# Scale and shift rows made side by side, biases in an early wait, and block 1's statistics ahead of the first queries, in the prologue of an adaLN attention + MLP kernel

## The chip, the cores and the metric

One core of a Trainium2 chip. The metric is the device time of one execution in microseconds (us), median of several executions. Engines are named as in the profile: PE is TensorE, DVE VectorE, ACT ScalarE, POOL GpSimd, SP the engine that issues nearly all DMAs.

## What is computed

One transformer layer on 2048 rows of width 512 in float32: attention with 32 query heads of 16 numbers that share one key head and one value head, then an MLP of width 1376. Both get their input through a layer norm whose scale and shift come from a vector `c`:

```python
mod = silu(c) @ w_mod                      # six rows of 512: sa, ca, ga, sb, cb, gb
h = layernorm(x) * (1 + ca) + sa
q, k, v = h @ wq, h @ wk, h @ wv           # 32 query heads, one key and value head
o = softmax(q @ k.T / 4) @ v               # for every head
x = x + ga * (o @ wo)
h = layernorm(x) * (1 + cb) + sb
out = x + gb * (gelu(h @ w1 + b1) @ w2 + b2)
```

## The kernel before

Attention is done in 64 units, each four heads of 256 query rows. The main loop (from `for u in range(NU)`) interleaves three things on PE: the scores of unit u (`e`, L685, exponentials on ACT in `p`), their product with the values (`acc`, L706), and, one to two units ahead, a first pass over the scores that only finds each row's maximum (`m`, L580, one `TENSOR_REDUCE` on DVE per product, L585). The rest (query projections, output projection, MLP) is fed in between in batches. The change leaves this loop alone.

All of the change is in the **prologue**, which ends where the first `e` product starts. Its order is written out by hand: each engine runs its instructions in the order of the code, and an engine whose next instruction waits holds up all that is behind it. x is worked in four blocks of 512 rows (`xt0` to `xt3`). Operands of accurate products are split in a high and a low part (`...H` on ACT, `...L` by subtraction on DVE or POOL), and a product is three matmuls: high by high, low by high, high by low.

The steps and their names:

- **Modulation rows.** `mod_row` (L308) multiplies `csb` (silu of c, 32 equal columns) with a half of a `w_mod` tile: `i` = 1 is the scale ca, `i` = 0 the shift sa. The two go to rows 32 to 63 and 0 to 31 of the bank `modrow`. ACT copies them to `modr` (L1373, L1384), `turn_rows` (L312) turns them to columns in `modc`. The scale half of `w_mod` is loaded ahead, the shift half after the first piece of `wq` (`load_mod`, L242). The scale is made first, then the shift, one matmul behind each row tile of block 0.
- **Block 0.** `stats1` (L406) makes mean and variance on DVE (`BATCH_NORM_STATS2`) and `rs`, `nm` on POOL; `xhat1` (L414) normalizes four tiles; `turn1` (L427) turns them by PE to the banks `tp`; `split1` (L433) makes `h0H`, `h0L`.
- **Biases.** `sab` holds the shift columns; `bias_row` (L370) multiplies it with `wq` and `wk`, giving the constant part of queries, keys and values (`biases`; for the other three query groups `bqs`, in `bias_rest`, L382, four matmuls of 384 columns).
- **First queries and keys.** `q_group` and `keys` (L1354, L1341) give the first 128 query columns (`qps`) and the keys and values of a block (`kps`). `place_q` (L532) puts the queries of unit 0 in place by selection products, `kv_out`, `low_k`, `repeat_k` (L451 to L468) write the keys to `ks` on ACT, DVE, ACT.
- **Blocks 1 to 3.** Normalized on ACT or POOL (`xhat1`), turned, copied from the bank by ACT (`x32`, L441), split by ACT and POOL (`bigH`, `bigL`).
- **Slots.** `SLOTS` (L25) is a table that sets the rest: a number n is n `m` products (`chunk`), a name is a step: "x 2" normalizes block 2, "heads 2" turns and splits one column tile of it, "keys 2" three matmuls of its keys, "low 2" and "k 2" the second and third write of the keys, "v 2" turns its values, "wq 1" scales and splits the second 128 query columns, "q 1" one quarter of the second queries, "rows" four modulation rows of the late part. From slot number `WIDE` on, every second `m` uses one of the three `e` banks; before that all `m` share three banks (tag "m", bufs=3), so the fourth `m` waits for the reduction of the first.

`FIRST_MAX` (L24) sets the order of the `m` products of units 0 and 1: (unit, key block) = (0,0), (1,0), (0,1), (1,1), (0,2), (0,3), (1,2), (1,3), eight products each. Only when all of unit 0's are reduced does `put_max` (L604) turn the maxima (DVE), gather and split them (POOL, `mt`, `mh`, `ml`) and send them by DMA into the rows of `qst` from which the first `e` products read. `keep_warm` (L290) issues matmuls on `wkH` whose results nobody reads.

Of the kernel before, what the change touches and what calls it, by code (L numbers as in the profile page):

```python
# [21 lines left out]
LEAD = 6  # L22
LEAD_0 = 6
FIRST_MAX = ((0, 0), (1, 0), (0, 1), (1, 1), (0, 2), (0, 3), (1, 2), (1, 3))  # L24
SLOTS = ((2, "x 2"), (2, "keys 1"), (2, "keys 1"), (2, "keys 1"), (2, "x 3", "keys 1"),  # L25
# [4 lines left out]
         (2, "rows"), (2, "rows", "wq 3"), (2, "rows", "load"), (2,))  # L30
WIDE = 16
MAX_WAIT = (1, 4)
QBUFS = 4
PREP = 4
# [22 lines left out]
def adaln_mqa_mlp(  # L57
# [182 lines left out]
    wms = [pro.tile([P, 2, D], F32, name=f"wm{k}", tag="wm", bufs=4) for k in range(KD)]  # L240

    def load_mod(i):  # L242
        for k in range(KD):
            nc.sync.dma_start(out=wms[k][:, i, :], in_=w_mod[k * P:(k + 1) * P, i * D:(i + 1) * D])

    load_mod(1)
# [17 lines left out]
    load_mod(0)  # L264
    load_x(1)
    load_x(2)
    load_x(3)
# [37 lines left out]
        for i, part in enumerate(wm):  # L305
            nc.tensor.matmul(ps[32 * i:32 * i + 32, :], csb[:, k, :], part, start=k == 0, stop=k == KD - 1)  # L306

    def mod_row(ps, i, k):  # L308

        nc.tensor.matmul(ps[32 * i:32 * i + 32, :], csb[:, k, :], wms[k][:, i, :], start=k == 0, stop=k == KD - 1)  # L310

    def turn_rows(ps, rows, i, n):  # L312
        for k in range(n):
            nc.tensor.transpose(ps[:, k, :], rows[32 * i:32 * i + 32, k * P:(k + 1) * P], ident[32 * i:32 * i + 32, 32 * i:32 * i + 32])

    pad(pro, 64, "pad2")
    wkH = pro.tile([P, KD, P], F32R, name="wkH")
# [29 lines left out]
    def scaled(dst, w, eng=nc.gpsimd):  # L347
        eng.tensor_tensor(out=dst, in0=w, in1=ca1.unsqueeze(2).to_broadcast([P, KD, P]), op=ALU.mult)
# [12 lines left out]
    def split_wq(g):  # L361
        gs = slice(g * P, (g + 1) * P)
        for j in range(2):
            src = wqms[g].rearrange("p k (a j r) -> p k a j r", j=2, r=16)[:, :, :, j, :]
            dh = wqH[:, :, gs].rearrange("p k (a r j) -> p k a j r", j=2, r=16)[:, :, :, j, :]
            dl = wqL[:, :, gs].rearrange("p k (a r j) -> p k a j r", j=2, r=16)[:, :, :, j, :]
            nc.scalar.copy(dh, src)
            nc.gpsimd.tensor_tensor(out=dl, in0=src, in1=raw(dh), op=ALU.subtract)

    def bias_row(ps, w):  # L370
        for k in range(KD):
            nc.tensor.matmul(ps, sab[:, k, :], w[:, k, :], start=k == 0, stop=k == KD - 1)

    def take_q(dst, ps):

        nc.scalar.copy(dst.rearrange("p (a r j) -> p a j r", j=2, r=16), ps.rearrange("p (a j r) -> p a j r", j=2, r=16))

    def prep_wq(g):
        scale_wq(g)
        split_wq(g)  # L380

    def bias_rest():  # L382

        n = KD - 1
        ps = psum.tile([P, n * P], F32, name="bqs", tag="x")
        row = pro.tile([32, n * P], F32, name="bqr", tag="h32", bufs=4)
        bias_row(ps[:32], wqf[:, :, P:D])
        for i in range(n):
            take_q(row[:, i * P:(i + 1) * P], ps[:32, i * P:(i + 1) * P])
# [24 lines left out]
    def xhat1(b, eng, n=QT):  # L414

        mv, rs, nm = hts_stats[b]
        xt = xts[b]
        for t in range(QT):
            eng = eng if t < n else nc.gpsimd
            if eng is nc.scalar:  # L420
                nc.scalar.activation(xt[:, t, :], xt[:, t, :], AF.Identity, scale=rs[:, t:t + 1], bias=nm[:, t:t + 1])
            else:
                eng.tensor_scalar(out=xt[:, t, :], in0=xt[:, t, :], scalar1=mv[:, t, 0:1], scalar2=rs[:, t:t + 1],
                                  op0=ALU.subtract, op1=ALU.mult)
            yield
# [7 lines left out]
    def split1(b, d):  # L433

        hH, hL = hts[b]
        ps = tps.pop((b, d))
        if b == 0:
            split(hH[:, d, :], hL[:, d, :], ps, act, dve)
        else:
            x32 = pro.tile([P, BQ], F32, name=f"x32_{b}_{d}", tag="h32", bufs=4)  # L440
            nc.scalar.copy(x32, ps)  # L441
            split(hH[:, d, :], hL[:, d, :], x32, act, pool)
# [927 lines left out]
    psc = psum.tile([P, 2, KD, 32], F32, name="modc", tag="v")  # L1370
    for k in range(KD):
        mod_row(psr, 1, k)
    nc.scalar.copy(modr[32:64], psr[32:64])  # L1373
    turn_rows(psc[:, 1], modr, 1, KD)
    nc.scalar.activation(ca1, psc[:, 1, :, 0], AF.Identity, bias=1.0)
    wqms[0] = pro.tile([P, KD, P], F32, name="wqm0", tag="wqm", bufs=1)
    for k in range(KD):
# [6 lines left out]
    nc.scalar.copy(modr[0:32], psr[0:32])  # L1384
    turn_rows(psc[:, 0], modr, 0, KD)
    spread_wkv()
    scaled(wkm, wk0, dve)
    load_constants()
    nc.vector.tensor_copy(out=sab, in_=psc[:, 0, :, 0:1].to_broadcast([P, KD, 32]))
    for d in range(KD):  # L1390
        split1(0, d)
    group = q_group()
    run(group, 1)
# [10 lines left out]
    nc.vector.tensor_copy(out=bq[:, 0:1], in_=psb[:, 2, 0:1])  # L1404
    nc.vector.tensor_copy(out=vbias, in_=psb[:, 3, 0:1])
    nc.vector.scalar_tensor_tensor(out=kbias, in0=psb[:, 3, 0:1], scalar=kkeep, in1=kmin, op0=ALU.mult, op1=ALU.add)

    def first_q(t):
        if t == 1:
            run(group)  # L1410
            load_q(1)

    stats1(1, first_q)
# [266 lines left out]
```

## Time and profile before

| | us |
|---|---|
| median of 3 runs (1571.49 to 1572.98) | 1572.91 |
| the profiled execution | 1574.09 |
| its span in the profile | 1572.3 |
| PE / DVE / ACT / POOL busy | 1556.0 / 1396.5 / 1232.0 / 680.6 |
| first `m` product starts | 31.62 |
| first `e` product starts (the prologue's end) | 91.52 |
| first `acc` product starts | 95.26 |

The profiled execution took 1.8 us more than its span, and 1.2 us more than the median of the runs. The prologue is 6% of the span; from 95 us on PE is busy in every stretch of 5 us. A row of the timeline has the start, the busy time of the group, engine, line, operation, tiles (out<-in), shapes and count, and in brackets the idle time of the engine just before it with what ended it. PEld is the load of a matmul's stationary operand.

### The profile page before, as it was taken

Reading aid. Unit: us, or ns where it says so; the run is one execution under the profiler, and the core shown is the slowest. Engines: PE = TensorE matmul, PEld = TensorE weight load, DVE = VectorE, ACT = ScalarE, POOL = GpSimd, SP = SyncE. Lnnn points to the kernel's source line nnn. Section 1 sums busy time; section 2 is a strip of 40 time slices with the busy share of each in tenths; the row PEclk is TensorE's granted clock in tenths of the full one; section 3 lists DMA queues with packets and bytes.
Section 4 is the critical chain, followed back from the end, with each engine's and each line's share of the span. In section 5 each row is a group of like instructions: output and inputs, shape, how many; then the busy total and the mean of one; then the engine's idle time right before and its main releaser. Section 6 shows DMA issues by size and latency. Waiting matters only on the chain.

```text
span 1572.3 us, 41712 instructions
## 1 busy us (share of the span) xinstructions
PE 1556.0 (99%) x16478; PEld 964.5 (61%) x16478; DVE 1396.5 (89%) x2490; ACT 1232.0 (78%) x2413; POOL 680.6 (43%) x1209
## 2 busy tenths in 40 slices
PE   8899999999999999999999999999999999999999
PEld 5445555556655676556655576556655676566658
DVE  5689999999999999999999999999999999999914
ACT  4657778778877888788877888778877888778874
POOL 3536452776521573235702474225721574146511
PEclk9999999999999999999999999999999999999999
DMA  7115521413112130302112130212202130203141
GB/s 255 66 47 178 179 79 54 144 47 98 45 48 79 45 98 16 110 17 87 55 42 86 35 107 17 86 51 62 89 26 76 45 116 26 83 28 100 48 148 48
DMA packets 83975, 120.65 MB, mean 77 GB/s; under 512 B 21294, under 2 KB 56686, under 8 KB 83524
## 3 DMA queue, kind: packets, MB, share of 16 engines
q1 hardware_dynamic: 83764, 117.99, 23.4%
q8 instruction: 130, 2.13, 0.6%
q14 instruction: 65, 0.53, 0.1%
q10 hardware_dynamic: 16, 0.00, 0.0%
HBM read 90.67 MB, written 26.74 MB: 75 GB/s over the span
## 4 chain that ended last, share of the span: by engine, by line
PE 87%; DVE 7%; DMA 0%; issue 0%; DVEq 0%; ACT 0%; SPq 0%
PE acc L706 30%; PE m L580 25%; PE e L685 16%; PE w1ps L202 8%; DVE mx L585 6%; PE w2ps L202 2%; PE w2ps L192 2%; PE qps L202 1%; PE w1ps L192 1%; PE wops L202 1%; PE tp L202 1%; DVE st L891 0%; PE wops L192 0%; DVE x L884 0%; PE modl L306 0%; DMA qst<-ml 0%
## 5 line engine op out<-in xcount | busy, mean ns | idle before, releaser
L585 DVE TENSOR_REDUCE mx<-m 128x1 f32<-128x512 f32 x2048 | 1270.7, 683 | 97.3 <-PE m L580 75.6
L689 ACT ACTIVATE p<-e 128x512 f32<-128x512 f32 x2048 | 1098.9, 598 | 255.8 <-PE e L685 107.5
L580 PE MATMUL m<-ks,qst 64*128 64x512 f32 x2048 | 835.0, 430 | 5.1 <-ACT va L477 2.2
L685 PE MATMUL e<-qst,ks 64*128 64x512 f32 x2048 | 740.0, 411 | 0.5 <-DMA qst<-ml 0.5
L706 PE MATMUL acc<-p,va 128*32 128x256 f32 x8192 | 548.0, 385 | 0.0
L580 PEld LDWEIGHTS m<-ks,qst 64*128 64x128 f32 x2048 | 366.8, 184 | 209.5 <-DVE mx L585 170.3
L685 PEld LDWEIGHTS e<-qst,ks 64*128 64x128 f32 x2048 | 359.1, 184 | 90.0 <-ACT p L689 62.8
L706 PEld LDWEIGHTS acc<-p,va 128*32 128x32 f32 x8192 | 213.8, 109 | 214.2 <-issue 111.0
L202 PE MATMUL w1ps<-h2H,w1t 64*128 64x256 f32 x1232 | 236.1, 288 | 0.0
L628 POOL TENSOR_SCALAR mt<-turned 8x32 f32<-8x32 f32 x256 | 53.2, 208 | 403.2 <-DVE turned L634 391.2
L202 PEld LDWEIGHTS w1ps<-h2H,w1t 64*128 64x128 f32 x1232 | 185.9, 185 | 28.9 <-issue 21.0
L202 PE MATMUL w1ps<-h2L,w1t 64*128 64x256 f32 x616 | 169.2, 275 | 0.0
L202 PE MATMUL w2ps<-w2H,gH 64*128 64x512 f32 x274 | 120.3, 439 | 0.0
L202 PEld LDWEIGHTS w1ps<-h2L,w1t 64*128 64x128 f32 x616 | 114.0, 185 | 0.0
L202 PE MATMUL w2ps<-w2L,gH 64*128 64x512 f32 x274 | 107.5, 392 | 0.0
L202 PE MATMUL w2ps<-w2H,gL 64*128 64x512 f32 x274 | 106.8, 390 | 0.0
L1043 POOL TENSOR_SCALAR tt<-tt 128x256 f32<-128x256 f32 x77 | 31.0, 403 | 130.5 <-ACT tt L1042 95.6
L144 POOL TENSOR_TENSOR gL<-z,gH 128x256 fp32r<-128x256 f32 x77 | 56.9, 739 | 6.4
L1044 POOL TENSOR_TENSOR tt<-tt,z 128x256 f32<-128x256 f32 x77 | 56.9, 739 | 6.4
L1054 POOL TENSOR_TENSOR z<-tt,z 128x256 f32<-128x256 f32 x77 | 56.4, 732 | 6.0
L1053 POOL TENSOR_TENSOR tt<-tt,z 128x256 f32<-128x256 f32 x77 | 56.9, 738 | 0.0
L202 PEld LDWEIGHTS w2ps<-w2H,gH 64*128 64x128 f32 x274 | 50.4, 184 | 6.6 <-issue 2.9
(221 smaller groups left out, 1532.4 us busy)
## 6 DMA issues: line engine op xcount, KB each, us to landing
w1t<-dw SPq DMA_DIRECT2D x82, 512.0 KB
qst<-dq SPq DMA_DIRECT2D x378, 32.0 KB
do<-oc SPq DMA_DIRECT2D x62, 128.0 KB
dw<-w1s SPq DMA_DIRECT2D x11, 512.0 KB
xt<-in_A_x_dram SPq DMA_DIRECT2D x4, 1024.0 KB
dq<-qH SPq DMA_DIRECT2D x16, 256.0 KB
dq<-qL SPq DMA_DIRECT2D x16, 256.0 KB
x<-in_A_x_dram SPq DMA_DIRECT2D x8, 512.0 KB
```

What stands on the lines that cost most here:

```text
L144: eng_l.tensor_tensor(out=dst_l, in0=src, in1=raw(dst_h), op=ALU.subtract)
L192: nc.tensor.matmul(ps, a, b_, start=first_, stop=last_)
L202: ins = nc.tensor.matmul(ps, a[rows], b_[rows], start=first_ and s == 0, stop=last_ and s == 1)
L580: nc.tensor.matmul(m, qsts[u][rows, j, t * P:(t + 1) * P], ks[rows, kc * 512:(kc + 1) * 512], start=True, stop=True)
L585: nc.vector.tensor_reduce(out=self.mx[u][:, i, kc:kc + 1], in_=m, axis=AX.X, op=ALU.max)
L628: nc.gpsimd.tensor_scalar(out=mt[:, g:g + 32], in0=turned[g:g + 4 * T, :], scalar1=1.0, scalar2=0.0, op0=ALU.mult, op1=ALU.add)
L685: nc.tensor.matmul(e, ks[rows, kt * P:(kt + 1) * P], rhs, start=True, stop=True)
L689: ins = nc.scalar.activation(dst, e, AF.Exp, scale=0.25)
L706: ins = nc.tensor.matmul(accs[u][32 * cidx:32 * cidx + 32, :], va[:, kt, :], rhs, start=kt == 0, stop=kt == NKT - 1)
L1044: nc.gpsimd.tensor_tensor(out=tt, in0=tt, in1=z, op=ALU.mult)
L1053: nc.gpsimd.tensor_tensor(out=tt, in0=tt, in1=z, op=ALU.mult)
L1054: nc.gpsimd.tensor_tensor(out=z, in0=tt, in1=z, op=ALU.add)
```

## The change

The diff, cut to its core:

```diff
-SLOTS = ((2, "x 2"), (2, "keys 1"), (2, "keys 1"), (2, "keys 1"), (2, "x 3", "keys 1"),
-         ("heads 2", "low 1", "k 1", "heads 2"), (2, "heads 2"), (2, "heads 2", "v 0"),
-         (2, "heads 3"), (2, "keys 2", "heads 3"), (2, "keys 2"), (2, "keys 2"), (2, "keys 2"), ("heads 3", "low 2", "k 2", "heads 3"),
-         (2, "wq 1", "keys 3"), (2, "v 1", "keys 3"), (4, "keys 3", "keys 3"),
-         ("q 1", "low 3", "k 3", "q 1"), (4, "q 1", "v 2", "q 1"), ("wq 2", "v 3"), (4, "rows"),
+SLOTS = ((2, "keys 1"), (2, "x 2", "keys 1"), (2, "keys 1"), (2, "keys 1"), ("x 3", "heads 2", 2, "low 1", "k 1", "heads 2"),
+         (2, "heads 2"), (2, "heads 2", "v 0"),
+         (2, "heads 3"), (2, "keys 2", "heads 3"), (2, "keys 2", "x2"), (2, "keys 2"), (2, "keys 2"), ("heads 3", "low 2", "k 2", "heads 3"),
+         (2, "wq 1", "keys 3", "v2"), (2, "v 1", "keys 3"), (4, "keys 3", "keys 3"),
+         ("low 3", "k 3", "v3"), (4, "q 1", "v 2", "q 1"), (4, "q 1", "v 3", "q 1"), ("wq 2",), (4, "rows"),
          (2, "rows"), (2, "rows", "wq 3"), (2, "rows", "load"), (2,))
-WIDE = 16
+WIDE = 15
...
+    for k in range(KD):
+        wm = pro.tile([P, 2, D], F32, name=f"wm{k}", tag="wm", bufs=4)
+        nc.sync.dma_start(out=wm, in_=w_mod[k * P:(k + 1) * P, 0:2 * D].rearrange("p (i n) -> p i n", i=2))
...
     for k in range(KD):
-        mod_row(psr, 1, k)
-    nc.scalar.copy(modr[32:64], psr[32:64])
-    turn_rows(psc[:, 1], modr, 1, KD)
-    nc.scalar.activation(ca1, psc[:, 1, :, 0], AF.Identity, bias=1.0)
-    wqms[0] = pro.tile([P, KD, P], F32, name="wqm0", tag="wqm", bufs=1)
-    for k in range(KD):
-        nc.scalar.activation(wqms[0][:, k, :], wqf[:, k, 0:P], AF.Identity, scale=ca1[:, k:k + 1])
-    split_wq(0)
+        mod_rows(psr, k, wms[k])
+    nc.scalar.copy(modr[:64], psr[:64])
     for t, _ in enumerate(xhat1(0, dve)):
+        if t == QT - 1:
+            turn_rows(psc, modr)
         for d in range(KD):
             turn1(0, d, [t])
-        mod_row(psr, 0, t)
-    nc.scalar.copy(modr[0:32], psr[0:32])
-    turn_rows(psc[:, 0], modr, 0, KD)
+    nc.scalar.activation(ca1, psc[:, :, 32], AF.Identity, bias=1.0)
+    scale_wq(0)
     spread_wkv()
+    nc.vector.tensor_copy(out=sab, in_=psc[:, :, 0:1].to_broadcast([P, KD, 32]))
     scaled(wkm, wk0, dve)
     load_constants()
...
     bias_row(psb[:32, 0, :], wqf[:, :, 0:P])
     bias_row(psb[:32, 1, :], wk0)
+    split1(0, 0)
+    split1(0, 1)
+    split_wq(0)
+    split1(0, 2)
+    split1(0, 3)
+    group = q_group()
+    run(group, 1)
...
-    def first_q(t):
+    def first_cols(t):
         if t == 1:
+            ...
+        elif t == QT - 1:
             run(group)
             load_q(1)
...
     keep_v(0)
+    bias_rest()
     def first_k(t):
-        if t == 1:
+        if t == QT - 1:
             low_k(0)
             repeat_k(0)
     stats1(2, first_k)
...
-    keep_warm(WARM[1], tag="x", bufs=1)
-    for t, _ in enumerate(xhat1(1, act)):
-        if t < 2:
-            chunk(2)
+    take_rest()
+    chunk(3)
+    for t, _ in enumerate(xhat1(1, act, 2)):
         for d in range(KD - 1):
             turn1(1, d, [t])
-        keep_warm(WARM[2], tag="x", bufs=1)
+        if t == 0:
+            chunk(1)
+            turn_rest()
+        keep_warm(WARM[2], tag="v", bufs=1)
     split1(1, 0)
     turn1(1, KD - 1)
+    chunk(2)
     split1(1, 1)
-    bias_rest()
+    split1(1, 2)
     stats1(3)
     load_mods(2)
-    split1(1, 2)
     split1(1, 3)
...
+            elif part in work:
+                next(work[part])
             else:
-                next(work[part])
+                keep_warm(int(part[1:]), tag=part[0], bufs=1)
```

`mod_rows` (already there for the late rows) issues one matmul for each half of a `w_mod` tile, the shift's to rows 0 to 31 of the bank and the scale's to rows 32 to 63, one behind the other. `xhat1(1, act, 2)` normalizes two row tiles of block 1 on ACT and the other two on POOL; before, all four were on ACT. `bias_rest` is cut in three: its products, the copies (`take_rest`) and the turns (`turn_rest`). A part such as "x2" in a slot now means two idle matmuls into the bank "x". Six `m` products instead of four are issued ahead of the slots, so 58 instead of 56 are done when the main loop starts, whose first step then issues 6 instead of 8; from there on all engines' orders are the same as before.

On DVE, the reductions of the first `m` products and the statistics of block 3, which read `xt_154` before and `xt_150` after. Before:

```order
L585 TENSOR_REDUCE mx_433<-m_0_1_0_1_453 128x1
L210 BN_STATS st<-xt_154 128x6 x4
L214 BN_AGGR mv<-st 128x2 x4
L216 TENSOR_SCALAR ve<-mv 128x4
L585 TENSOR_REDUCE mx_433<-m_1_0_0_0_529 128x1
L585 TENSOR_REDUCE mx_433<-m_1_0_0_1_532 128x1
```

After:

```order
L588 TENSOR_REDUCE mx_422<-m_0_1_0_1_439 128x1
L588 TENSOR_REDUCE mx_422<-m_1_0_0_0_479 128x1
L588 TENSOR_REDUCE mx_422<-m_1_0_0_1_482 128x1
L210 BN_STATS st<-xt_150 128x6 x4
L214 BN_AGGR mv<-st 128x2 x4
L216 TENSOR_SCALAR ve<-mv 128x4
L588 TENSOR_REDUCE mx_422<-m_1_1_0_0_516 128x1
```

The statistics now stand behind the fifth and sixth reduction, and the seventh waits behind them.

On ACT, around the keys of block 1 (`kps1`): `xt2`, `xt3` are the rows of blocks 2 and 3 being normalized, `x32_2_0` the first column tile of block 2. Before:

```order
L421 ACTIVATE xt2_152<-xt2_152,nm2_414,rs_412 128x512 x4
L421 ACTIVATE xt3_154<-xt3_154,nm3_516,rs_514 128x512 x2
L453 ACTIVATE ks_81<-kps1_545,cols_73 128x512
L441 COPY x32_2_0_587<-tp2_0_582 128x512
L139 CAST bigH_193<-x32_2_0_587 128x512
L466 CAST ks_81<-ks_81 16x512
```

After:

```order
L424 ACTIVATE xt2_148<-xt2_148,nm2_408,rs_406 128x512 x4
L456 ACTIVATE ks_81<-kps1_522,cols_73 128x512
L424 ACTIVATE xt3_150<-xt3_150,nm3_507,rs_505 128x512 x2
L444 COPY x32_2_0_568<-tp2_0_563 128x512
L139 CAST bigH_189<-x32_2_0_568 128x512
L469 CAST ks_81<-ks_81 16x512
```

Block 3's two row tiles moved behind the first write of block 1's keys, and still stand ahead of block 2's first copy and of the last write of those keys.

On PE, from the last product of block 3's keys to the first of the second queries (`qps0_1`); an `m` is named m, unit, half, row tile, key block, side. Before:

```order
L169 MATMUL kps3_738<-bigL_194,wkH_169 128x512
L169 MATMUL qps0_1_776<-h0H_195,wqH_189 128x512
L169 MATMUL qps0_1_776<-h0H_195,wqL_190 128x512
L169 MATMUL qps0_1_776<-h0L_196,wqH_189 128x512
L169 MATMUL qps0_1_776<-h0H_195,wqH_189 128x512
```

After:

```order
L169 MATMUL kps3_728<-bigL_190,wkH_165 128x512
L293 MATMUL idle6_773<-wkH_165 128x512 x3
L583 MATMUL m0_1_1_2_0_777<-ks_81,qst0_153 128x512
L583 MATMUL m0_1_1_2_1_780<-ks_81,qst0_153 128x512
L583 MATMUL m0_0_0_3_0_783<-ks_81,qst0_153 128x512
L583 MATMUL m0_0_0_3_1_786<-ks_81,qst0_153 128x512
L169 MATMUL qps0_1_789<-h0H_191,wqH_185 128x512
```

Ahead of the second queries now stand three idle matmuls and four `m` products, the last two of which read block 3's keys (key block 3).

More of the change, by code (lines that the diff above doesn't have):

```diff
@@ L239, in adaln_mqa_mlp @@
     load_x(0)
-    wms = [pro.tile([P, 2, D], F32, name=f"wm{k}", tag="wm", bufs=4) for k in range(KD)]
-    def load_mod(i):
-        for k in range(KD):
-            nc.sync.dma_start(out=wms[k][:, i, :], in_=w_mod[k * P:(k + 1) * P, i * D:(i + 1) * D])
-    load_mod(1)
+    wms = []
+    for k in range(KD):
+        wm = pro.tile([P, 2, D], F32, name=f"wm{k}", tag="wm", bufs=4)
+        nc.sync.dma_start(out=wm, in_=w_mod[k * P:(k + 1) * P, 0:2 * D].rearrange("p (i n) -> p i n", i=2))
+        wms.append([wm[:, i, :] for i in range(2)])
     wkv = pro.tile([P, KD, 2 * Dh], F32, name="wkv")
@@ L263, in adaln_mqa_mlp @@
     nc.sync.dma_start(out=wqf[:, :, 0:P], in_=wqr[:, :, 0:P])
-    load_mod(0)
     load_x(1)
@@ L306, in mod_rows, with turn_rows @@
             nc.tensor.matmul(ps[32 * i:32 * i + 32, :], csb[:, k, :], part, start=k == 0, stop=k == KD - 1)
[L308 to L314, printed above, removed]
+    def turn_rows(ps, rows):
+        for k in range(KD):
+            nc.tensor.transpose(ps[:, k, :], rows[:64, k * P:(k + 1) * P], ident[:64, :64])
     pad(pro, 64, "pad2")
@@ L380, in prep_wq, with take_rest, turn_rest @@
         split_wq(g)
+    rest_q = {}
     def bias_rest():
         n = KD - 1
-        ps = psum.tile([P, n * P], F32, name="bqs", tag="x")
-        row = pro.tile([32, n * P], F32, name="bqr", tag="h32", bufs=4)
+        ps = rest_q["ps"] = psum.tile([P, n * P], F32, name="bqs", tag="x")
+        row = rest_q["row"] = pro.tile([32, n * P], F32, name="bqr", tag="h32", bufs=4)
         bias_row(ps[:32], wqf[:, :, P:D])
-        for i in range(n):
-            take_q(row[:, i * P:(i + 1) * P], ps[:32, i * P:(i + 1) * P])
+    def take_rest():
+        for i in range(KD - 1):
+            take_q(rest_q["row"][:, i * P:(i + 1) * P], rest_q["ps"][:32, i * P:(i + 1) * P])
+    def turn_rest():
+        n = KD - 1
+        ps, row = rest_q["ps"], rest_q["row"]
         for i in range(n):
@@ L1369, in adaln_mqa_mlp @@
     psr = psum.tile([P, D], F32, name="modrow", tag="x")
-    psc = psum.tile([P, 2, KD, 32], F32, name="modc", tag="v")
+    psc = psum.tile([P, KD, 64], F32, name="modc", tag="v")
     for k in range(KD):
-        mod_row(psr, 1, k)
-    nc.scalar.copy(modr[32:64], psr[32:64])
-    turn_rows(psc[:, 1], modr, 1, KD)
-    nc.scalar.activation(ca1, psc[:, 1, :, 0], AF.Identity, bias=1.0)
-    wqms[0] = pro.tile([P, KD, P], F32, name="wqm0", tag="wqm", bufs=1)
-    for k in range(KD):
-        nc.scalar.activation(wqms[0][:, k, :], wqf[:, k, 0:P], AF.Identity, scale=ca1[:, k:k + 1])
-    split_wq(0)
+        mod_rows(psr, k, wms[k])
+    nc.scalar.copy(modr[:64], psr[:64])
     for t, _ in enumerate(xhat1(0, dve)):
+        if t == QT - 1:
+            turn_rows(psc, modr)
         for d in range(KD):
             turn1(0, d, [t])
-        mod_row(psr, 0, t)
-    nc.scalar.copy(modr[0:32], psr[0:32])
-    turn_rows(psc[:, 0], modr, 0, KD)
+    nc.scalar.activation(ca1, psc[:, :, 32], AF.Identity, bias=1.0)
+    scale_wq(0)
     spread_wkv()
+    nc.vector.tensor_copy(out=sab, in_=psc[:, :, 0:1].to_broadcast([P, KD, 32]))
     scaled(wkm, wk0, dve)
     load_constants()
[L1389 to L1393, printed above, removed]
     psb = psum.tile([P, 4, P], F32, name="biases", tag="m", bufs=3)
@@ L1403, in adaln_mqa_mlp @@
         nc.tensor.transpose(psb[:, 2 + i, :32], rowb[:, i, :], ident[:32, :32])
-    nc.vector.tensor_copy(out=bq[:, 0:1], in_=psb[:, 2, 0:1])
-    nc.vector.tensor_copy(out=vbias, in_=psb[:, 3, 0:1])
-    nc.vector.scalar_tensor_tensor(out=kbias, in0=psb[:, 3, 0:1], scalar=kkeep, in1=kmin, op0=ALU.mult, op1=ALU.add)
-    def first_q(t):
+    def first_cols(t):
         if t == 1:
+            nc.vector.tensor_copy(out=bq[:, 0:1], in_=psb[:, 2, 0:1])
+            nc.vector.tensor_copy(out=vbias, in_=psb[:, 3, 0:1])
+            nc.vector.scalar_tensor_tensor(out=kbias, in0=psb[:, 3, 0:1], scalar=kkeep, in1=kmin, op0=ALU.mult, op1=ALU.add)
+        elif t == QT - 1:
             run(group)
             load_q(1)
-    stats1(1, first_q)
+    stats1(1, first_cols)
     keys0 = keys(0)
```

## The prediction

> **What bounds the kernel now.** First the page's busy times and the shares of the chain that ended last:
>
> ```profile
> PE 1556.0 (99%) x16478; PEld 964.5 (61%) x16478; DVE 1396.5 (89%) x2490; ACT 1232.0 (78%) x2413; POOL 680.6 (43%) x1209
> PE 87%; DVE 7%; DMA 0%; issue 0%; DVEq 0%; ACT 0%; SPq 0%
> ```
>
> PE bounds the kernel, and its 16 us of idle time lie nearly all in the prologue. From the first `e` product on, every engine's order stays what it was but for two `m` products fewer in the first step, so the main loop should keep its length: the change is worth what it moves that product. Then the prologue's timeline, for what each stage waits on:
>
> ```profile
> 14.69 1.05 PE L310 MATMUL modrow<-wm,csb 128*32 128x512 f32 x2
> 18.90 0.57 ACT L1384 COPY modr<-modrow 32x512 f32<-32x512 f32 x1 [4.01 <-PE modrow L310]
> 21.37 1.06 PE L372 MATMUL biases<-wqf,sab 128*32 128x128 f32 x8
> 25.07 0.50 PE L169 MATMUL qps<-h0H,wqH 128*128 128x512 f32 x1
> 31.62 0.49 PE L580 MATMUL m<-ks,qst 64*128 64x512 f32 x1 [0.98 <-DVE ks L457]
> 70.07 0.49 PE L169 MATMUL qps<-h0H,wqH 128*128 128x512 f32 x1 [1.25 <-ACT wqH L367]
> 75.56 0.69 ACT L508 ACTIVATE q<-qps,cols 128x512 f32<-128x512 f32 x1 [0.68 <-PE qps L169]
> 80.14 0.79 PE L580 MATMUL m<-ks,qst 64*128 64x512 f32 x1 [2.18 <-ACT va L477]
> 85.41 1.03 POOL L628 TENSOR_SCALAR mt<-turned 8x32 f32<-8x32 f32 x4 [4.13 <-DVE turned L634]
> 91.52 0.59 PE L685 MATMUL e<-qst,ks 64*128 64x512 f32 x2
> ```
>
> The shift rows end at 18.9 and hold the biases; these the last first queries (three products from 25.07); these the first `m` (31.62). The second queries end at 75.5, unit 0's maxima reach POOL at 85.41, and `e` starts at 91.52.
>
> The clock is read from the table of stretches of 1 us (start:end, length, PE busy and count, granted clock, DMA share, GB/s):
>
> ```profile
> 53.00:54.00 1.00, 0.92 (x6) 0.50 0.69 139
> 79.00:80.00 1.00, 0.00 (x0) 0.95 0.70 262
> 80.00:81.00 1.00, 0.86 (x5) 0.50 0.00 0
> 86.00:87.00 1.00, 1.00 (x10) 0.63 0.00 0
> ```
>
> Twice the clock falls to 0.50: at 53, and from 79.9 to 86.7, some 6.8 us, right behind the wait of 2.18 us quoted above. What that costs, two products one behind the other show:
>
> ```profile
> 23.58 0.40 PE L169 MATMUL qps<-h0H,wqL 128*128 128x512 f32 x1
> 23.82 0.39 PE L169 MATMUL qps<-h0L,wqH 128*128 128x512 f32 x1
> 55.59 0.63 PE L169 MATMUL kps<-bigH,wkL 128*128 128x512 f32 x1
> 56.02 0.63 PE L169 MATMUL kps<-bigL,wkH 128*128 128x512 f32 x1
> ```
>
> From start to start 0.24 us at full clock, 0.43 at half: 0.19 more for each.
>
> **The front part.** The four shift matmuls behind the tiles of block 0 (1.05 us each) go; one now stands beside each scale matmul. No row shows such a pair; the nearest are the late rows:
>
> ```profile
> 76.48 1.06 PE L306 MATMUL modl<-wml,csb 128*32 128x512 f32 x8
> 80.86 1.93 PE L306 MATMUL modl<-wml,csb 128*32 128x512 f32 x8
> ```
>
> Four matmuls (8 records) on four column groups take 1.06 us, what one (2 records) takes alone. So they lie side by side, and I take 1.0 for a pair. Bounds: no more than one, or two in a row, 0.6 more a pair by their pitch and +1.9 us over the last ones. But the rows now need both halves of `w_mod`:
>
> ```profile
> 0.00:5.00 5.00, 3.19 (x15) 1.00 0.52 123
> 5.00:10.00 5.00, 5.00 (x32) 1.00 1.12 344
> 10.00:15.00 5.00, 4.33 (x19) 1.00 1.07 375
> ```
>
> Up to 10 us 0.62 + 1.72 = 2.3 MB have come. x's first block (1.05 MB) and the two halves (2.1) make 3.15, so the last is there at 10 + 0.85 / 0.375 = 12.3, with the small loads 12.6, and the rows are done at 13.6 instead of 18.87. ACT's copy (0.57), four turns and DVE's copy to `sab` take it to about 15.6; the biases run there, where PE has nothing else. What then decides are the weights and `h0L`:
>
> ```profile
> 68.22 1.04 POOL L348 TENSOR_TENSOR wqm<-wqf,ca 128x512 f32<-128x512 f32 x1
> 14.16 0.73 ACT L367 CAST wqH<-wqm 128x256 fp32r<-128x256 f32 x2
> 69.78 1.43 POOL L368 TENSOR_TENSOR wqL<-wqm,wqH 128x256 fp32r<-128x256 f32 x2 [0.53 <-ACT wqH L367]
> 20.20 2.48 DVE L144 TENSOR_TENSOR h0L<-tp,h0H 128x512 fp32r<-128x512 f32 x4
> ```
>
> Columns are there at about 15.1, and POOL's scaling (1.04), ACT's high part (0.73) and POOL's low part (1.43) end by 18.4; `h0L`, behind `sab` and the scaled keys' weights (0.7 us) on DVE, by 18.9. Eleven products of 0.24 and two small turns later, near 22.0, the first queries are done, instead of 26.0. **Gain here: 4.0 us**, first `m` at 27.7. `bias_rest` takes the place of the six idle products ahead of it. All four tiles of block 2's statistics, not two, now precede the second write of block 0's keys on DVE; ACT's copy of the values hides them, and without that cover they cost 1.3 us. On SP four DMA issues go, and the rest of `wq` lands a little ahead of its use.
>
> **Given back at block 1.**
>
> ```profile
> 32.24 2.93 ACT L421 ACTIVATE xt<-xt,nm,rs 128x512 f32<-128x512 f32 x4
> 45.49 4.15 POOL L423 TENSOR_SCALAR xt<-xt,mv,rs 128x512 f32<-128x512 f32 x2
> 36.52 0.59 ACT L441 COPY x<-tp 128x512 f32<-128x512 f32 x1 [1.34 <-PE tp L431]
> 35.80 2.46 DVE L210 BATCH_NORM_STATS2 st<-xt 128x6 f32<-128x512 f32 x4
> 48.18 0.78 ACT L453 ACTIVATE ks<-kps,cols 128x512 fp32r<-128x512 f32 x1
> 50.11 0.62 ACT L466 CAST ks<-ks 16x512 fp32r<-16x512 f32 x1
> ```
>
> A row tile takes 0.73 us on ACT, 2.08 on POOL. POOL's two start near 29.5 behind its own `nm` and end at 33.7; block 1's first copy follows at 34.2 instead of 36.52, so 2.4 of the 4.0 us are left. Then DVE: six reductions stand ahead of block 3's statistics (2.46, and 0.55 for what follows them), the seventh behind. `m` has three banks, so the ninth `m` at the latest waits for a reduction behind the statistics, and the products of block 1's keys stand behind it in PE's queue. I make that a hole in PE's work of some 3 us, about 37.9 to 40.9: the wait that the early statistics were to hide has become a new one. It is longer than the 2.18 us ahead of 79.9, so I expect the clock to fall near 40. The keys of block 1, twelve products and ten `m` in their midst, then end at about 46.6; at full clock 44.7; before 48.14.
>
> Behind them ACT first writes these keys (0.78), then normalizes two tiles of block 3 (1.5 us, which stood ahead of it before), then copies and splits block 2's first tile (1.2): the last write is at 50.1, where it was. **Gain that is left: 0.2 us**, for a pair of `m` that is issued already; 1.9 at full clock.
>
> In blocks 2 and 3 the idle pair in the middle of `keys 2` costs 0.46 us at full clock and 0.87 at half: **0.7 lost**. The idle pair in `keys 3` lies in a wait for POOL's `bigL`; without that cover it costs the same.
>
> **Second queries.** B is the end of POOL's last `bigL`, 66.97 + 1.29 = 68.26.
>
> ```profile
> 66.97 1.29 POOL L144 TENSOR_TENSOR bigL<-x,bigH 128x512 fp32r<-128x512 f32 x1 [1.34 <-PE m L580]
> 71.60 0.62 ACT L466 CAST ks<-ks 16x512 fp32r<-16x512 f32 x1 [0.81 <-DVE ks L457]
> ```
>
> The last write of block 3's keys ends at 72.22 = B + 3.96, and nothing ahead of it changes. Now two `m` that read these keys stand ahead of the first of the second queries in PE's queue. From B + 4.0 on PE has twelve products (2.9 us), six `m` (0.22 each) and two sets of turns (0.35 each): the last ends at about B + 9.35, against B + 7.3 (75.5) before. **2.1 lost.** Bounds: 0.3 less, since the old order waited for the weights anyway; 3.3 more if the clock falls (below).
>
> **The end.** "v 3" now stands ahead of "wq 2", so the wait of 2.18 us at 80.14 goes: `va` stood on ACT behind a `wqH` that waits for POOL. And all of unit 0's `m` come ahead of the late rows, so its maxima are reduced while POOL is still busy:
>
> ```profile
> 76.97 1.27 POOL L144 TENSOR_TENSOR qL<-q,qH 128x512 fp32r<-128x512 f32 x1 [5.76 <-ACT qH L139]
> 81.13 0.16 POOL L101 MEMSET pad<- 128x64 f32 x1
> L685 PEldq EVENT_SEMAPHORE  x128: 51/51/178, 90.5 to 1504.5; - x128
> ```
>
> X is the end of the second queries (75.53). POOL's `qL`, scaling, `wqL` and memset end at 81.29 = X + 5.75, and then it stood idle 4.13 us, for maxima that came last and at half clock. Now the gather can start right there. From gather to the release of `e` (the wait of PE's weight queue at 90.5) it is 5.1 us, to `e` itself 6.1, because idle matmuls were still running; I take 5.2. So `e` starts at X + 11.0 instead of X + 16.0: **5.0 gained**. Bounds: 4.1 with the 6.1; 0 if unit 0's maxima still come last.
>
> **Sum.** 0.2 - 0.7 - 2.1 + 5.0 = 2.4 us gained: 1571.7 from the profiled execution's 1574.09. The median of the runs is 1.2 lower: 1570.5, with 0.8 to 1 either way from the idle pair, the 5.2 and the 2.1: 1568.5 to 1572.5.
>
> **Rivals.** *The clock stays full behind the hole at 38.* Keys 1 then end 1.9 us earlier, and the half-clock stretch at 53 need not come either, which cost block 2 about 2.2 in its twelve products: 1566.4. For it: the hole is only about 3 us, and some of it may hide in the six `m` ahead. Against it: 2.18 us were enough at 79.9. The Trainium skill, "TensorE: Matmul & The Clock Gate", section "Why this matters for your kernels", warns of PE-idle gaps over about 3 us between bursts; by that this hole might just pass and the time would be this rival's. The fall behind 2.18 us in the row at 80.14 speaks against so long a limit.
>
> *The clock falls ahead of the second queries: the slower one.* From B + 0.5 to B + 4.0 PE has three idle products and two `m`, 1.2 us of work in 3.5, while the writes of block 3's keys run. Before, products of the second queries lay in that place. If so little work lets the clock fall, it falls just as the twelve products and six `m` start: 18 × 0.19 = 3.4 us, 1573.9; and if it still lasts when the late rows run (1.93 instead of 1.06, four times), up to 1577.4. It decides once the share of work in that stretch is as small as ahead of 79.9, where PE did nothing from 78 to 80. For it: the work is a third. Against it: the three idle products split the wait.
>
> *An early fall.* At 13.8 to 16 PE only turns tiles. If the clock falls there, some 25 products of first queries and keys cost 0.19 more: +4.8, 1575.3. The same page of the Trainium skill, section "Part 4: PE-mode transpose", says that transposes do not count as PE activity in the same way. No row here has a stretch of turns alone to test it.
>
> *The rows don't run side by side*: two in a row, +1.9 us as bounded above: 1572.4.
>
> **How the numbers follow.** Chances: forecast 0.37; full clock behind the hole 0.21; fall ahead of the second queries 0.29; early fall 0.08; rows in a row 0.05. 0.2%, about what a measurement of this kernel can tell from no change, is 3.1 us. Under 1569.8 lie the second case, 0.21, and a third of the forecast's, 0.12: faster 0.33. Over 1576.0 lie half of the third, 0.14, half of the early fall, 0.04, and 0.02 of the forecast's for maxima that come last: slower 0.20. Same: 0.47. The range reaches from a little below the full clock's 1566.4 to the third case's upper end: 1565 to 1577.
>
> **What would show it.** Rows done at 13.6; first `m` near 27.7; PE waiting 2 to 3 us on DVE ahead of block 1's keys, and a clock of 0.50 behind it; the last second query at B + 9.35; no wait on `va`; `e` 11.0 us behind the last second query, with POOL no longer waiting for `turned`. The forecast is wrong if the falls of the clock lie elsewhere, if the biases still hold the first queries, or if POOL still waits for unit 0's maxima.

## The result and the profile after

| | before | changed |
|---|---|---|
| median of 17 runs each, us | 1573.61 (1571.40 to 1576.56) | 1576.39 (1575.05 to 1578.02) |
| ratio of the times, 95% interval | | 1.0016 (1.0009 to 1.0024) |
| span of the profiled execution, us | 1572.3 | 1575.1 |
| half-clock time in it up to 104 us | 13.7 | 27.3 |
| mean granted clock of the runs | 0.9958 (23 runs) | 0.9914 (17 runs) |

The kernel became slower by 2.5 us (1.4 to 3.8), where 2.4 us of gain were forecast (1570.5). The forecast's range (1565 to 1577) holds the time; its direction was wrong. Half-clock time is summed from the table of 1 us stretches; a stretch at 0.75 counts half. The 23 runs are those of the kernel before that were timed beside experiments 1 to 4. One slow execution of the end-only kernel (4487 us, experiment 4) is in no number here.

The shortest way to the loss is one question to each trace: PE's stretches between the same six events (start:end, length, PE busy and count, granted clock, DMA share, GB/s). The ends are the first `m`, the first write of block 1's keys, the end of the last `bigL`, the end of the second queries, the first `e`, and 20 us more. Before:

```profile
0.00:31.62 31.62, 27.25 (x132) 1.00 0.80 254
31.62:48.18 16.56, 14.84 (x63) 1.00 0.54 198
48.18:68.26 20.08, 19.45 (x85) 0.83 0.16 54
68.26:75.53 7.27, 5.31 (x23) 1.00 0.00 0
75.53:91.52 15.99, 12.90 (x62) 0.79 0.12 40
91.52:111.52 20.00, 19.89 (x190) 1.00 0.18 49
```

After:

```profile
0.00:27.97 27.97, 24.46 (x130) 1.00 0.87 286
27.97:47.74 19.77, 15.62 (x56) 0.79 0.47 168
47.74:70.54 22.80, 20.06 (x82) 0.80 0.14 47
70.54:81.89 11.35, 10.66 (x44) 0.88 0.00 0
81.89:92.34 10.45, 8.64 (x53) 1.00 0.15 54
92.34:112.34 20.00, 19.26 (x160) 0.83 0.08 19
```

The front is 3.65 us shorter and the end 5.5. The three stages between are longer by 3.2, 2.7 and 4.1, and in each the clock is below 1.00. Up to `e` that makes 0.8 us lost. The last row shows the rest: the span grew by 2.8, so 2.0 us are lost behind `e`, in an order unchanged but for two `m` fewer, where the clock was 1.00 before and is 0.83 now.

The front and the end, on the engine and line named in each row:

```profile
12.36 1.05 PE L303 MATMUL modrow<-wm,csb 128*32 128x512 f32 x4 [0.60 <-DMA wm<-in_w_mod_dram]
15.85 1.06 PE L365 MATMUL biases<-wqf,sab 128*32 128x128 f32 x8
27.97 0.73 PE L583 MATMUL m<-ks,qst 64*128 64x512 f32 x3
34.18 0.59 ACT L444 COPY x<-tp 128x512 f32<-128x512 f32 x1 [2.45 <-PE tp L434]
87.67 1.03 POOL L631 TENSOR_SCALAR mt<-turned 8x32 f32<-8x32 f32 x4
```

The pair takes 1.05 us, as long as one alone: the rows do lie side by side, done at 13.4, with `w_mod` the last to come. The biases run at 15.85. POOL's gather has no wait ahead of it any more. Between them lie these:

```profile
37.15 2.46 DVE L210 BATCH_NORM_STATS2 st<-xt 128x6 f32<-128x512 f32 x4
40.73 0.79 PE L583 MATMUL m<-ks,qst 64*128 64x512 f32 x1 [2.23 <-DVE mx L588]
50.64 0.74 DVE L460 SCALAR_TENSOR_TENSOR ks<-kps,cols,ks 16x512 fp32r<-16x512 f32 x1
51.41 0.62 ACT L469 CAST ks<-ks 16x512 fp32r<-16x512 f32 x1 [0.37 <-DVE ks L460]
51.43 0.49 PE L583 MATMUL m<-ks,qst 64*128 64x512 f32 x1 [1.46 <-DVE ks L460]
67.97 0.73 PE L293 MATMUL idle<-wkH 128*128 128x512 f32 x2 [1.13 <-ACT vt L465]
92.34 0.59 PE L688 MATMUL e<-qst,ks 64*128 64x512 f32 x2 [1.81 <-DMA qst<-ml]
93.78 0.75 PE L583 MATMUL m<-ks,qst 64*128 64x512 f32 x1 [0.74 <-ACT modl_sb L1468]
```

Four waits of PE: on the reductions behind block 3's statistics, on the second write of block 1's keys, on an idle pair's own bank, and of `e` on unit 0's maxima. In the kernel before, the second write of block 1's keys followed the first (48.18) without a reduction between them:

```profile
48.99 0.74 DVE L457 SCALAR_TENSOR_TENSOR ks<-kps,cols,ks 16x512 fp32r<-16x512 f32 x1 [0.43 <-ACT ks L453]
```

The clock falls four times, inside the first of these waits and behind each of the others (start:end, length, busy time and count of PE, PEld, DVE, ACT and POOL, then the granted clock, DMA share, GB/s):

```profile
39.00:40.00 1.00, 0.00 (x0) 0.00 (x0) 0.96 (x8) 1.00 (x2) 0.25 (x1) 0.62 0.72 303
49.00:50.00 1.00, 0.98 (x6) 0.53 (x4) 0.69 (x2) 1.00 (x3) 0.00 (x0) 0.76 0.00 0
53.00:54.00 1.00, 1.00 (x5) 0.35 (x3) 0.30 (x1) 0.97 (x3) 0.00 (x0) 0.50 0.00 0
59.00:60.00 1.00, 1.00 (x6) 0.70 (x4) 0.43 (x1) 0.00 (x0) 1.00 (x1) 0.64 0.28 115
70.00:71.00 1.00, 1.00 (x4) 0.43 (x4) 0.46 (x1) 0.00 (x0) 1.00 (x2) 0.50 0.00 0
73.00:74.00 1.00, 1.00 (x5) 0.77 (x5) 0.89 (x2) 0.00 (x0) 0.49 (x1) 0.81 0.00 0
94.00:95.00 1.00, 1.00 (x6) 0.80 (x6) 0.44 (x1) 1.00 (x3) 0.00 (x0) 0.50 0.16 51
100.00:101.00 1.00, 1.00 (x8) 0.76 (x8) 0.87 (x2) 0.60 (x1) 0.00 (x0) 0.66 0.00 0
```

Half clock from 39.3 to 49.5, 52.9 to 59.7, 70.0 to 73.4 and 93.9 to 100.7: 27 us, against two falls and 13.7 us before.

These places belong to this one execution. The kernel of experiment 1 has the same order up to the idle products ahead of `e`, and its profile has the same three waits (2.24, 1.57 and 1.13 us) and 27.3 us of half clock. But there the falls begin at 31.1, 41.3, 51.6 and 95.9, and none stands behind the 1.13. The total varies less than the places: the 17 runs of the changed kernel have mean clocks of 0.990 to 0.993.

### The profile page after: what moved, and what is told of

Same layout as the page of the kernel before. It is cut to its first block, busy times and chain, and to the rows that moved or that the text cites. A ratio compares the mean times of both kernels' runs of the same rounds, so it can differ in the third digit from the quotient of the medians.

```text
span 1575.1 us, 41698 instructions
## 1 busy us (share of the span) xinstructions
PE 1557.5 (99%) x16475; PEld 967.6 (61%) x16475; DVE 1397.0 (89%) x2490; ACT 1229.4 (78%) x2406; POOL 685.4 (44%) x1212
## 4 chain that ended last, share of the span: by engine, by line
PE 89%; DVE 7%; POOL 1%; issue 1%; DMA 1%; ACT 0%; SPq 0%; ACTq 0%; DVEq 0%; POOLq 0%
PE acc L709 30%; PE m L583 25%; PE e L688 16%; PE w1ps L202 8%; DVE mx L588 6%; PE w2ps L202 2%; PE w2ps L192 2%; PE qps L202 1%; PE w1ps L192 1%; PE wops L202 1%; PE tp L202 1%; PE kps L169 1%; DMA wm<-in_w_mod_dram 1%; PE tp L434 0%; DVE st L894 0%
```

## The experiments

**Theory 1**: front and end bring what was forecast; the middle's new waits take it back, twice over, as waits and as half clock behind them. **Theory 2**: the waits or the queue orders alone are the price, and the clock is a mark of them. All kernels were timed in turns with the kernel before; "before" is its median in the same set, and the ratio stands with its 95% interval. The numbers are those of the order in which they ran, which the expectations use.

**2. Statistics early.** Block 3's statistics go ahead of the fifth reduction, where DVE waits 4.7 us for PE.

```diff
+    stats1(3)
     split1(1, 0)
     turn1(1, KD - 1)
     chunk(2)
     split1(1, 1)
     split1(1, 2)
-    stats1(3)
```

> The changed kernel with block 3's statistics issued ahead of the fifth reduction, in a stretch where DVE waits 4.7 us for PE. Theory 1 (the hole at 38.4 to 40.7 comes from the statistics on DVE, and the clock falls because of it): the hole goes, no half clock from 39.4 to 49.8, block 1's keys end near 42.5 instead of 47.5, and of these 5 us 3 or more arrive at e: 1572 to 1573.5 in all. Theory 2 (what decides is the order on ACT and POOL behind it, xt2 and xt3 ahead of the repeated keys): the hole goes, but the repeated keys come under 1.5 us earlier, 1575 to 1576.

Measured: 1571.00, before 1574.01, ratio 0.9972 (0.9962 to 0.9983): 5.4 us under the changed kernel by the medians, 6.9 by the two ratios to the kernel before. The hole is gone, PE is busy throughout where it stood:

```profile
37.00:42.00 5.00, 5.00 (x19) 1.00 0.58 220
```

Block 1's keys are written at 42.23 instead of 47.74, and `e` starts at 87.0 instead of 92.3. Its profile has 17.1 us of half clock instead of 27.3. Theory 1 holds, by more than it had said; the order behind it on ACT did not take the gain back. So the place of four statistics instructions on DVE costs more than the whole change loses.

**6. Idle products in the hole.** This parts the hole's own time from the clock behind it.

```diff
-SLOTS = ((2, "keys 1"), (2, "x 2", "keys 1"), (2, "keys 1"), ...
+SLOTS = ((2, "keys 1"), (1, "x10", 1, "x 2", "keys 1"), (2, "keys 1"), ...
```

> The changed kernel with ten idle products in the hole of 38.4 to 40.7: the wait stays, but PE has work in it. Theory 1 (half clock is what the hole costs, besides its 2.2 us): no fall near 39, block 1's keys end near 45 instead of 47.5, some 3 us less half clock cost in all, 1573.5. Theory 2 (the wait itself is the cost): 1576.4, no change.

Measured: 1573.11, before 1573.96, ratio 0.9992 (0.9983 to 1.0001): 3.3 us under the changed kernel by the medians, 3.8 by the ratios. The hole's place, and the `m` that waited:

```profile
39.65 2.55 PE L293 MATMUL idle<-wkH 128*128 128x512 f32 x10
42.12 0.50 PE L583 MATMUL m<-ks,qst 64*128 64x512 f32 x1
38.40:42.00 3.60, 3.60 (x14) 1.00 0.63 255
```

Counted from the `m` ahead of it, this `m` comes as late as in the changed kernel (4.2 us against 4.05), the products nobody reads fill PE, and behind them the clock stays at 1.00. Theory 1 said 1573.5, theory 2 1576.4: by the medians, more than half of what the early statistics win (5.4 us) comes without a shorter wait, from the clock; the other 2 to 3 us go with the wait. The runs' mean clock agrees, 0.9953 against 0.9914. How much of this belongs to the hole alone is not shown, since this profile has no fall behind the later waits either, though they are still there:

```profile
49.20 0.49 PE L583 MATMUL m<-ks,qst 64*128 64x512 f32 x1 [1.57 <-DVE ks L460]
63.46 0.73 PE L293 MATMUL idle<-wkH 128*128 128x512 f32 x2 [1.14 <-ACT vt L465]
```

**11. A wait of the kernel before, filled.** The same test without the change, at the wait of 2.18 us of before.

```diff
-         (2, "rows"), (2, "rows", "wq 3"), ...
+         (1, "v9", 1, "rows"), (2, "rows", "wq 3"), ...
```

> The kernel before with nine idle products in the wait of 2.18 us ahead of the m at 80.14. The wait stays. Theory 1 (such a wait lowers the clock, and two windows of half clock cost some 2 us): no fall at 80, unit 0's maxima and e some 2 us earlier, 1572. Theory 2 (the wait itself is the price): 1574, no change.

Measured: 1571.99, before 1575.41 (mean of its runs 1574.2), ratio 0.9986 (0.9975 to 0.9998). The late rows, which took 1.93 us there, behind the nine idle products:

```profile
78.88 2.37 PE L296 MATMUL idle<-wkH 128*128 128x512 f32 x9
81.18 0.49 PE L580 MATMUL m<-ks,qst 64*128 64x512 f32 x1
81.60 1.06 PE L306 MATMUL modl<-wml,csb 128*32 128x512 f32 x8
```

Nine products of no use make the kernel 2.2 us faster (0.3 to 3.9), and the mean clock of its runs is 0.9976 against 0.9951: theory 1 again. One profile alone would not show it: the falls at 52.6 and 79.9 are not there, but two of one step each stand at 33.9 and 71.5, where the order is that of before.

**7. Keys first.** On top of the early statistics, the second and third write of block 1's keys ahead of block 2's first copy and of two `m`.

```diff
-... ("x 3", "heads 2", 2, "low 1", "k 1", "heads 2"), ...
+... ("x 3", "low 1", "k 1", "heads 2", 2, "heads 2"), ...
```

> Statistics early as in the second experiment, and in the slot behind block 1's keys their second and third write ahead of block 2's first copy and of the two m's reductions. In that experiment's trace PE waits 1.57 and 0.52 us there, and the clock falls behind it from 46.3 to 56.6. Theory 1 (that wait lowers the clock): repeated keys at 44.4 instead of 45.5, the wait 1 us shorter, and with it one or two of the three windows of half clock gone: 1568 to 1570. Theory 2 (only the 1.1 us, or nothing): 1570 to 1571.

Measured: 1567.93, before 1573.96, ratio 0.9964 (0.9951 to 0.9978); the mean of its runs (1568.4) lies 2.5 us under that with the statistics alone (1570.9). The last write is at 44.18 instead of 45.55, PE's two waits there are 0.19 and 0.77 us instead of 1.57 and 0.52, and the half clock behind them ends at 53.6 instead of 56.7. So far it is as theory 1 said. But the two ratios' intervals overlap, and the fall at `e` is one step longer here, so that both profiles hold 17.1 us of half clock: how the gain divides between the wait and the clock is not shown.

**5. Front only.** The front of the change, and blocks 1 to 3 and the end as before.

```diff
 (against the changed kernel: SLOTS and WIDE of before, and)
     take_rest()
-    chunk(3)
-    for t, _ in enumerate(xhat1(1, act, 2)):
+    turn_rest()
+    for t, _ in enumerate(xhat1(1, act)):
+        if t < 2:
+            chunk(2)
         for d in range(KD - 1):
             turn1(1, d, [t])
...
-    chunk(2)
     split1(1, 1)
-    split1(1, 2)
     stats1(3)
     load_mods(2)
+    split1(1, 2)
```

> The front of the change alone (rows side by side, biases early, block 2's statistics ahead), with blocks 1 to 3 and the end in the order of the kernel before; the turns of the other query groups' biases stand ahead of the first m, which costs some 0.7 us. Theory 1 (the front's 4 us are real and are lost behind it to the new waits and the half clock they bring): first m near 28.7, block 1's first copy near 33.5, block 1's keys 3 us earlier than before, 1570 to 1571.5 in all. Rival (a front that is earlier only makes what follows wait longer, on x's loads or the statistics, so little of it arrives): block 1's keys under 1 us earlier, 1573 to 1574.

Measured: 1569.17, before 1573.96, ratio 0.9965 (0.9952 to 0.9977). First `m` at 29.03, block 1's keys written at 42.30 instead of 48.18: 5.9 us earlier, since the other groups' biases no longer stand ahead of these keys either. The rival (an early front only makes the rest wait) falls.

**4. End only.** The kernel before with the end's order of the change, less its three idle products.

```diff
-         ("q 1", "low 3", "k 3", "q 1"), (4, "q 1", "v 2", "q 1"), ("wq 2", "v 3"), (4, "rows"),
-         (2, "rows"), (2, "rows", "wq 3"), (2, "rows", "load"), (2,))
+         ("low 3", "k 3"), (4, "q 1", "v 2", "q 1"), (4, "q 1", "v 3", "q 1"), ("wq 2",), (4, "rows"),
+         (2, "rows"), (2, "rows", "wq 3"), (2, "rows", "load"))
```

> The kernel before with nothing but the end's order of the change: four m ahead of the first of the second queries, v 3 ahead of wq 2. The prediction's terms for it: 5.0 us gained from the second queries' end to e, 2.1 lost ahead of the second queries: e 2.9 us earlier, 1570.7, if the clock holds. Rival (the clock falls ahead of the second queries, or behind e's wait where 9 idle products end too early): no gain, 1573.6 or more.

Measured: 1572.25, before 1574.01, ratio 0.9987 (0.9976 to 0.9997). From the last `bigL` to the end of the second queries, and on to `e`:

```profile
68.47:77.81 9.34, 8.42 (x32) 0.82 0.00 1
77.81:88.86 11.05, 8.61 (x53) 1.00 0.16 56
```

20.4 us instead of 23.3: the forecast's 9.35 and 11.0. That the first fits is luck, since it holds a fall of the clock that the forecast did not put there. Behind `e` the clock falls again, at 89.9. Of the 2.9 us some 2.0 arrive, an amount (0.5 to 3.8) that can't be told from all of them.

**9, 10, 12. Front and end**, the middle of before; then the same with 17 idle products ahead of `e`, and with two of block 1's row tiles on POOL.

```diff
 (front only, with the end's order:)
+         ("low 3", "k 3", "v3"), (4, "q 1", "v 2", "q 1"), (4, "q 1", "v 3", "q 1"), ("wq 2",), (4, "rows"),
+         (2, "rows"), (2, "rows", "wq 3"), (2, "rows", "load"))
 (second:)
-WARM = (20, 6, 2, 9)
+WARM = (20, 6, 2, 17)
 (third:)
-    for t, _ in enumerate(xhat1(1, act)):
+    for t, _ in enumerate(xhat1(1, act, 2)):
```

> Front and end of the change, blocks 1 to 3 in the order of the kernel before, without the idle pairs. Theory 1 (front and end are gains, the middle is the loss): the fifth experiment's 1569.2 less the 2.9 us from the last bigL to e that the fourth one's trace shows, less some half clock behind e's wait: 1566.5 to 1567.5. Rival (at the end the clock takes back all that the order gives): 1569 or more.

> The same with 17 instead of 9 idle products ahead of e. Theory 1 (the empty PE ahead of e lowers the clock behind it): no fall at the main loop's start, 1 to 2 us under the run beside it. Against it: the first and third experiments had 17 and their profiles show a fall there all the same; then no difference.

> Front and end as in the first of this set, and block 1's third and fourth row tile on POOL, as the change has them. A tile takes 2.08 us on POOL and 0.73 on ACT. Theory 1 (POOL's two, one after the other, are the longer path): block 1's first copy 0.5 to 1 us later than with four on ACT, 0.5 to 1 us slower. Rival (the earlier ACT lets the fourth tile and the keys start sooner): as fast or faster.

Measured, before 1575.41 (mean of its runs 1574.2): 1565.32, ratio 0.9933 (0.9921 to 0.9946); 1563.82, 0.9926 (0.9913 to 0.9939); 1564.32, 0.9932 (0.9919 to 0.9944). Front and end together are worth 10.5 us (8.5 to 12.4), more than expected, and this is **the fastest order found, with either number of idle products**. The three times can't be told apart. With the rows on POOL block 1's first copy is at 35.24 instead of 33.48, though 0.25 us of that is there at the first `m` already, and this profile has a fall at 30.7 that the other has not; what it costs at the end is less than these runs can show, so sharing the rows is neither the loss nor a gain that can be seen.

What the middle's order costs without any fall can be read here: from the first write of block 1's keys to that of block 2's, all at full clock. First in the order of the change (the kernel with idle products in the hole):

```profile
46.21:60.17 13.96, 11.88 (x60) 1.00 0.23 77
```

Then in that of before (front and end):

```profile
43.65:55.13 11.48, 10.64 (x56) 1.00 0.28 93
```

2.5 us more for the same keys: PE waits 2.1 us (the 1.57, and 0.52 on the third write) instead of 0.8, and an idle pair and one more pair of `m` run in between. The pair of `m` is work done earlier and not lost.

**8. Without the idle pairs.** The early statistics, less the pairs in `keys 2` and `keys 3`.

```diff
-... (2, "keys 2", "x2"), ...
+... (2, "keys 2"), ...
...
-... (2, "wq 1", "keys 3", "v2"), ...
+... (2, "wq 1", "keys 3"), ...
```

> Statistics early as in the second experiment, without the idle pairs in keys 2 and keys 3. The pair in keys 3 sits 1.12 us waiting for its bank behind the copy of block 2's values, with m products behind it whose keys are there 0.7 us sooner. Theory 1: the pairs cost 0.46 and 1.2 us, 1.5 us less in all: 1569.5. Rival (they are what keeps the clock up through keys 2 and keys 3): a fall more, 1571 to 1573.

Measured: 1572.36, before 1573.96, ratio 0.9989 (0.9979 to 0.9998); the mean of its runs is 1.0 us above that with the pairs. The last `bigL` ends at 64.07 instead of 66.16, but then:

```profile
68.00:75.00 7.00, 6.92 (x18) 0.51 0.00 0
```

A fall over most of the stage from there to the end of the second queries (76.46), which the run with the pairs does not have. It went the rival's way: the pairs cost their time and pay it back. The intervals overlap a little (0.9979 to 0.9998, 0.9962 to 0.9983), and there is one profile of each, so it is likely rather than shown.

**1, 3. More idle products ahead of `e`**, in the changed kernel, and with the early statistics. Each has 17 for 9 in `WARM`, as above.

> The changed kernel with 17 instead of 9 idle products ahead of the first e. In its trace PE has nothing from 90.5 to 92.3, and the clock is 0.50 from 93.9 to 100.7, where the kernel before keeps 1.00; from e to the end it takes 2.0 us more. Theory 1 (the idle time ahead of e lowers the clock, and that costs the main loop's start): no fall at 94, the first acc about 1 us earlier (96.2), the time 1.5 to 2.0 us under the changed kernel (1574.4 to 1574.9). Theory 2 (the later e alone carries the loss, the clock there costs nothing on the path): no change, 1576.4.

> Both edits together: 17 idle products ahead of e and block 3's statistics ahead of the fifth reduction. Theory 1: the gains add, 1570 to 1572, under the kernel before. Theory 2: 1575 or more.

Measured: 1575.41, before 1574.01, ratio 1.0009 (0.9998 to 1.0020), which can't be told from the changed kernel's 1.0016; and 1571.11, 0.9965 (0.9953 to 0.9978), no different from the early statistics with 9. The wait ahead of `e` shrank from 1.81 to 0.64 us, and the clock fell all the same (the first of the two):

```profile
92.97 0.59 PE L688 MATMUL e<-qst,ks 64*128 64x512 f32 x2 [0.64 <-DMA qst<-ml]
96.00:97.00 1.00, 1.00 (x3) 0.50 0.00 0
```

So theory 1 in this form falls: that the empty PE ahead of `e` brings this fall was argued only, and filling most of it does not remove it. The fall goes with the end's order as a whole: in all eleven profiles of kernels with that order one begins between 0.1 us ahead of the first `e` and 3.1 us behind it, and in the three with the end of before (before, and experiments 5 and 11) none does. Which of its waits brings it stays open.

## Why the prediction was wrong

Of the 5.2 us between the forecast gain (2.4) and the loss in the span (2.8), blocks 1 to 3 make 1.8, the second queries 2.0 and the main loop 2.0; the end gives 0.5 back. Point by point, by the prediction's own steps:

- **The front**: forecast 4.0 gained, first `m` at 27.7; measured 27.97, 3.65 gained. Right: rows side by side, 12.6 for the load and 15.6 for `sab` within 0.4 us, and no early fall. The gain depends on the execution of before that it is taken from, since its front put the first `m` at 32.48 and 33.12 in experiments 11 and 4. The front-only kernel shows that the gain is real.
- **Block 1**: forecast a hole from 37.9 to 40.9 and a fall near 40; measured 38.5 to 40.73 and 39.3. Place and mechanism right. The fall lasted 10.2 us, longer than the two of before (6.8 each). That this comes from the hole's end, which leaves PE busy for 0.58 of the first 3.4 us of it, is argued only.
- **The keys' last write**, "at 50.1, where it was": measured 51.41, 1.3 us later. Most of it is the first write, at 47.74, where the prediction has the keys end at 46.6; from there ACT needs 3.3 us, about as forecast, and then waits 0.37 for DVE. What the step left out is the second write: it now stands on DVE behind two reductions, at 50.64 instead of 48.99, and PE waits 1.46 us for it. The keys-first kernel takes that back.
- **Blocks 2 and 3**, "0.7 lost": up to the end of the last `bigL` 2.3 us are lost in all, where the forecast has 0.5. The step priced the idle pair alone. A second fall came at 52.9, behind that wait, and even without a fall the new order takes 2.5 us longer than the old one from block 1's keys to block 2's (experiments 6 and 9), an idle pair and a pair of `m` that would come later among it. The pair in `keys 3`, which the prediction put under cover, waited 1.13 us for its own bank, and in this execution the clock fell behind it at 70.0.
- **Second queries**, "2.1 lost": 4.1, because that fall lies over the last products of block 3's keys. It is the slower rival's mechanism, by a wait 4 us earlier than the one it named, at 2.0 us instead of its 3.4. At full clock the stage takes 8.55 us (front and end), 1.3 more than before, so the 2.1 was too large for a stage without a fall.
- **The end**, "5.0 gained": 5.5, POOL's gather without a wait. Right.
- **"The main loop should keep its length"**: it lost 2.0 us, with a fall at 93.9. No case of the prediction had a fall behind `e`, which every profile of the end's order has. (The prediction's "nearly all in the prologue" for PE's 16 us of idle time is too strong: 11.9 lie ahead of 95 us, 3.2 at the very end. No term rests on it.)

What failed is thus the number of falls and the short waits: the sum moved one of two falls of the clock and kept their number. The change replaces long waits by more, shorter ones, which the prediction left out or priced as waits only. Half-clock time doubled, and the falls lay elsewhere, which the prediction had named as a sign of being wrong. What that is worth can be estimated from the runs of the kernel before alone, whose time follows their own mean clock: among 23, those with 0.992 took 1576.6 and 1576.9, the one with 1.000 took 1568.6, a fit 0.97 us for each 0.001. The changed kernel's runs have 0.0044 less: 4.3 us by that slope, so at equal clock it would be 1.8 us faster than before, near the 2.4 forecast. That is an estimate across kernels; the idle products in the hole show directly that filling a wait alone wins 3.3 us.

## What to carry to other kernels

Behind an early gain on a queue written out by hand, look for the first place where the new order lets an engine with few banks wait on a longer neighbour: here the statistics between two reductions cost 5 us and more, twice what the change lost, and they had free room a few rows ahead. Price a wait of the matrix engine as its length plus the half clock that may follow it, and try a change's parts apart before judging the whole: the same front and end with the old middle are 10 us faster than either kernel.

## What the runs showed of the hardware

In each of the fourteen profiles the granted clock changes on one grid of 3.41 us, and the half-clock stretches of the prologue are one, two or three steps long (3.4, 6.8, 10.2 us). The grid's phase differs from execution to execution, so the same order of work has its falls at different places (before at 52.6 and 79.9; with only the wait at 80 filled, at 33.9 and 71.5).

From 8 us to 107 us these profiles have 35 falls. Each follows a step with PE busy for 0.22 to 0.84 of it, 24 of them one with 0.67 or less; none of the some 230 steps with more than 0.85 was followed by a fall. Yet steps of 0.45 (83.0 to 86.4 in experiment 6) and 0.61 (27.0 to 30.4 in experiment 9) passed without one. So idle time makes a fall likely, and no threshold was found that decides it. The Trainium skill, "TensorE: Matmul & The Clock Gate", section "Why this matters for your kernels", warns of PE-idle gaps over about 3 us; here a wait of 2.23 us and, with smaller gaps beside them, waits of 1.46 and 1.13 us came with falls, so shorter gaps than that can be enough, while waits of 1.57 and 1.14 us passed without one in experiment 6.

With the clock goes the spread of one kernel's times: 1568.5 to 1577.4 for the kernel before, wider than the whole effect of this change.
